# One work list for a skewed Fourier convolution: groups overlapped sequence by sequence

## The chip, the cores and the metric

The kernel runs on one core of one Trainium2 chip. The core has a matrix engine (PE, with PEld for its weight loads), a vector engine (DVE), a scalar engine (ACT), a general engine (POOL) and a queue engine (SP); DMA queues are issued from SP, POOL and ACT. The metric is the device time of one execution in microseconds (us). Before the change it is 2036.44 us, the median of three runs (2035.06 to 2037.47).

## The reference, cut to what matters

The work is a long causal convolution over 5696 positions for 8 sequences and 128 channels, followed by a token-mixing block. Its second part takes the first part's output as x.

```python
def _attn_ref(x, h):                       # x (8, 5696, 128), h (5696, 128)
    B, S, D = x.shape
    L = 2 * S
    Xf = np.fft.rfft(x, n=L, axis=1)
    Hf = np.fft.rfft(h, n=L, axis=0)
    return np.fft.irfft(Xf * Hf[None], n=L, axis=1)[:, :S, :]

def _moe_ref(x, w_theta, w_tok_r, w_tok_i, w_ch):
    theta = x @ w_theta
    zr, zi = x * np.cos(theta), x * np.sin(theta)
    y = np.einsum('ts,bsd->btd', w_tok_r, zr) + np.einsum('ts,bsd->btd', w_tok_i, zi)
    u = x + y
    return u + np.maximum(u @ w_ch, 0.0)
```

## The kernel before, in words

The convolution is computed as matrix products with tables of sines and cosines, in float16. The 8 sequences and 128 channels are cut into eight groups (`groups`): two sequences times 64 channels each, first the four pairs of sequences for the lower channels (dh = 0), then for the upper (dh = 1). A group goes through four stages, each a list of steps. A step fills one PSUM tile `ps` (two banks; there are four such tiles, so all eight banks) and copies it out.

- Stage A (`stage_a`, line 239): 16 steps of 4 matmuls of 180 columns, table `f1_t` times the loaded `x16`. Each result is copied to the tile `a` by ACT (line 258) or, for steps named in `on_dve`, by DVE (line 256).
- Stage B (`stage_b`, line 392): 12 steps (11 of 8 frequencies, one of 2). `f2` (line 261) makes the spectrum of both sequences e in one `ps`; ACT copies it to a tile `xs` (line 399; two buffers); DVE multiplies it with the real and the imaginary part of the filter's spectrum, held in `hs` tiles, into `u_t` and `v_t` (line 401). So `u_t` holds both sequences' products with one part of the filter, `v_t` with the other. In the last step `f2` issues twelve further matmuls (`WARM`, line 275) whose results nobody reads.
- Stage C (`stage_c`, line 411): 16 steps of 8 pairs of matmuls, table `r_u` with `u_t` and `r_v` with `v_t`; steps 0 to 7 belong to the first sequence of the pair, 8 to 15 to the second. The result is multiplied by a table of signs and halves, `sgn`, on its way to the tile `g`: on DVE in one instruction (line 429), or on ACT in two (lines 426 and 427).
- Stage D (`stage_d`, line 432): 7 steps (six of 10 positions, one of 4), table `e_t` times `g`, copied by ACT to `yt` (line 447). The last step stores `yt` to `yt_hbm` through SP (line 453).

There is one buffer each of `a`, `g`, `yt` and `x16`, and one pair `u_t`, `v_t`. The loop over groups (line 755) weaves stage C of group g with stage A of group g+1, and then stage B of group g+1 with stage D of group g (`woven` sorts the steps of several lists by a position in each). Stage C of g+1 can begin only when stage B of g+1 has written all of `u_t` and `v_t`, and stage B only when stage C of g has read all of them. When A has taken its last input, POOL loads the next group's `x16` (16 DMAs, line 138). In group 3's stage B, SP refills each `hs` tile with the upper channels' spectrum from `hf_hbm` (lines 405 to 408).

The order of the instructions on an engine is set in one of two ways. Inside `tc.manual_schedule` (here `in_order`) DVE and ACT take their instructions as the program writes them. Outside it, and always for PE, a planner orders them from its own costs and readiness. `in_order` ends after stage C of group 0 (line 770).

Group 7 has no following group. Its stages C and D are woven with the first steps of the phases (`phase_step`, line 715), which turn `yt_hbm` into the sines and cosines of the second part. They use small tables `ones`, `pm` and `w_neg`, made in `open_phases` (line 640) while group 6 is worked on, and `ya0`, loaded by POOL from `yt_hbm` (line 653). After the spectrum of group 7, the ring for the token-mixing weights takes the place of the table `w_t2` (`open_ring`, line 609). From about 400 us the mixing products (line 1262 above all) fill the rest of the time.

Of the kernel before, what the change touches and what calls it, by code (L numbers as in the profile page):

```python
# [23 lines left out]
def kernel(  # L24
# [42 lines left out]
    w_ch_sb = const_pool.tile([P, P], BF16)  # L67

# [9 lines left out]
    NF = 2 * S  # L78
    N2 = 64
    N1 = NF // N2  # L80
    NB = S // N2
    K1 = N1 // 2 + 1
    KH = K1 // 2
    CK = 8
    HD = D // 2
    EN = N2 // 2 + 1
    WARM = 12
    XP = HD + 4
    assert N1 * N2 == NF and NB * N2 == S and NB % 2 == 1 and K1 <= P
# [4 lines left out]
    UVW = 2 * HD * K1  # L94
# [9 lines left out]
    conv, setup, xa, xin, pha = (ExitStack() for _ in range(5))  # L104
# [10 lines left out]
    fs = pool("fft_s", 2, conv, side="right")  # L115
    fy = pool("fft_y", 1, conv, side="right")
    s1 = pool("set_1", 1, setup, side="right")

    u_t = fc.tile([P, UVW + P], F16)
    v_t = fc.tile([P, UVW + P], F16)  # L120
    uv = [t[:, :UVW].rearrange("p (e d k) -> p e d k", e=2, k=K1) for t in (u_t, v_t)]
    h16 = s1.tile([P, 2, N2, HD], F16)
    for p0, p1 in ((0, 80), (80, NB)):
        nc.gpsimd.dma_start(u_t[p0:p1, :N2 * D],
                            bass.AP(tensor=h.tensor, offset=h.offset + p0 * N2 * D,
                                    ap=[[N2 * D, p1 - p0], [1, N2 * D]]))
# [25 lines left out]
    nc.vector.memset(lane[0:64, 2:3], 0.0)  # L152
    nc.vector.memset(lane[64:P, 2:3], float(KH))

# [64 lines left out]
    nc.vector.tensor_scalar(lane[:, 3:4], lane[:, 0:1], 1.0 / NF, None, op0=mult)  # L219
# [6 lines left out]
    nc.vector.tensor_scalar(f_t, f_k, lane[:NB, 1:2], 1.0 / N1, op0=mult, op1=mult)  # L226
# [15 lines left out]
    def stage_a(lhs, on_dve=()):  # L242
# [3 lines left out]
        def chunk(q):  # L246
# [8 lines left out]
            if q // 4 in on_dve:  # L255
                nc.vector.tensor_copy(a_out, a_in)
            else:
                nc.scalar.activation(a_out, a_in, AF.Copy)
        return [lambda q=q: chunk(q) for q in range(0, HD, 4)], st

    def f2(a_st, c, warm=True):
# [11 lines left out]
        if c == NCK - 1 and warm:  # L273
            for n in range(WARM):
                nc.tensor.matmul(ps[:, n % 2, ck * HD:ck * HD + 384], w_t2[:, 2, :P],
                                 w_t2[:, 0:2, :].rearrange("p k n -> p (k n)"), start=True, stop=True)
# [14 lines left out]
    for d0 in range(0, HD, 32):  # L291
        nc.vector.tensor_copy(h16[:NB, :, :, d0:d0 + 32],
                              u_t[:NB, :N2 * D].rearrange("p (n h d) -> p h n d", h=2, d=HD)[:, :, :, d0:d0 + 32])
    steps, a_h = stage_a(lambda q: h16[:NB].rearrange("p h n d -> p (h n) d")[:, :, q], (4, 6, 8, 10, 12, 14))
    w_rest(1)
    for f in steps:
        f()
    w_rest(2)

    nc.gpsimd.memset(u_t[:, UVW:], 0.0)  # L300
    nc.gpsimd.memset(v_t[:, UVW:], 0.0)
# [22 lines left out]
    def h_chunk(c):  # L324
        c0, ck = CHK[c]
        ps = f2(a_h, c, False)
        nc.scalar.activation(h_part(c)[:, 0], ps[:, 0], AF.Copy, scale=16.0 / NF)
        nc.vector.tensor_scalar(h_later[:, HD * c0:HD * (c0 + ck)].rearrange("p (d k) -> p d k", k=ck),
                                ps[:, 1], 16.0 / NF, None, op0=mult)
# [13 lines left out]
    sgn = fc.tile([P, N2], F32)  # L343

    def r_table(n_, r_):
# [10 lines left out]
        nc.scalar.activation(r_[:, :N2 + EN], k[:, :N2 + EN], AF.Copy, scale=0.125)  # L356
        nc.scalar.activation(r_[:, N2 + EN:], k[:, N2 + EN:], AF.Copy, scale=-0.125)
# [7 lines left out]
    def e_pair(n, cn):  # L365
        at = e_more if n % 4 == 3 else e_all[:, 2 * (n % 4) * ES * NB:]
        return [at[:K1, q * ES * NB:][:, :cn * NB] for q in range(2)]

    def e_index(n, n0, cn):
        t, k = e_pair(n, cn)  # L370
        index(k, [[1, cn], [N2, NB]], n0)
        nc.gpsimd.tensor_scalar(t, k, lane[:K1, 1:2], 1.0 / NF, op0=mult, op1=mult)
        up(t, k, nc.gpsimd)

    def e_table(n, n0, cn):
# [4 lines left out]
        sine(e_t[:K1, n0:n0 + cn, 1, :], t3, -1)  # L380
        cosine(e_t[:K1, n0:n0 + cn, 0, :], k3)

    def s_table():
        half, end = lane[:, 5:6], lane[:, 6:7]
        nc.vector.tensor_scalar(half, lane[:, 1:2], 0.0, -0.5, op0=ALU.is_equal, op1=mult)
        nc.vector.tensor_scalar(end, lane[:, 1:2], float(K1 - 1), -0.5, op0=ALU.is_equal, op1=mult)
# [938 lines left out]
```

## Time and profile before

| | us |
|---|---|
| median of three runs | 2036.44 |
| the profiled execution | 2035.64 |
| its span | 2033.9 |
| PE busy | 1936.4 |
| DVE busy | 1573.3 |
| POOL busy | 964.0 |
| ACT busy | 655.1 |
| first stage A matmul of group 2 | at 108.34 |
| first matmul of the phases | at 334.98 |

The profile holds one execution. A busy PE is a modelled figure, because matmuls are pipelined, so the distance from one start to the next says more than a sum of durations. A group of instructions is written as line, engine, operation, output tile, input tile, shape and count; behind the bar stand the total busy time, the mean duration in nanoseconds, and the idle time of the engine just before them with what ended it. On one engine the next instruction often starts a little before the one before it ends, so the pitch is shorter than the duration.

### The profile page before, as it was taken

To read this page: it belongs to the slowest core of one execution; us is meant where nothing else is said; L and a number is where in the kernel's file an instruction comes from. 1 tells how busy PE (TensorE), PEld (TensorE's weight loads), DVE (VectorE), ACT (ScalarE), POOL (GpSimd) and SP (SyncE) were. 2 spreads that over 40 slices of the span, in tenths; PEclk is the share of its full clock that TensorE was granted. 3 is DMA by queue.
4 is the path that set the end of the run, shared out by engine and by line. 5 is a ranking of instruction groups with operands and counts; after the bars stand their busy time and mean duration, and the time that the engine had idled before them with its cause. 6 is when DMAs were issued, how large, how long until landed. Compare 5 with 4: busy or idle time off the path is not lost.

```text
span 2033.9 us, 41286 instructions
## 1 busy us (share of the span) xinstructions
PE 1936.4 (95%) x15664; PEld 1073.2 (53%) x15841; DVE 1573.3 (77%) x2890; ACT 655.1 (32%) x1004; POOL 964.0 (47%) x1721
## 2 busy tenths in 40 slices
PE   6799999788999999999999999999999999999998
PEld 5688888654444444444444444444444444444444
DVE  8777778786788888888877669768677786777767
ACT  6788888851232323333210000011111111111111
POOL 8523322363364545455565554553545445354450
PEclk9799999998999999999999999999999999999999
DMA  9978975997898998989999899887878878788793
GB/s 115 64 84 124 89 87 165 266 272 139 163 174 177 174 178 154 180 170 181 171 168 164 121 241 243 131 149 129 152 135 146 149 129 144 137 146 147 133 157 85
DMA packets 487752, 312.05 MB, mean 153 GB/s; under 512 B 182887, under 2 KB 448615, under 8 KB 486567
## 3 DMA queue, kind: packets, MB, share of 16 engines
q0 software_dynamic: 321600, 155.29, 60.8%
q1 hardware_dynamic: 158784, 140.34, 24.0%
q10 hardware_dynamic: 7168, 13.76, 1.9%
q8 instruction: 124, 2.03, 0.4%
q14 instruction: 76, 0.62, 0.1%
HBM read 354.37 MB, written 90.29 MB: 219 GB/s over the span
## 4 chain that ended last, share of the span: by engine, by line
PE 66%; DMA 3%; DVE 3%; issue 1%; POOL 0%; ACT 0%; DVEq 0%; ACTq 0%
PE m L1262 62%; DMA b<-z_hbm 2%; DVE c L1269 1%; PE v L942 1%; PE utp L935 1%; PE m L1266 1%; PE m L1150 1%; DVE wt L855 1%; PE theta_ps L515 0%; PE tpz L883 0%; DMA yT<-yt_hbm 0%; PE m L1183 0%; POOL ring L631 0%; DMA ring<-in_moe_w_tok_r_dram 0%; DMA ring<-in_moe_w_tok_i_dram 0%
## 5 line engine op out<-in xcount | busy, mean ns | idle before, releaser
L631 POOL DMA_DIRECT2D ring<-in_moe_w_tok_i_dram x720 | 390.2, 552 | 652.8 <-DVE wt L855 554.0
L855 DVE STREAM_TRANSPOSE wt<-ring 128x384 f32<-128x384 f32 (+2 forms) x720 | 358.9, 523 | 115.1 <-PE m L1262 63.7
L631 POOL DMA_DIRECT2D ring<-in_moe_w_tok_r_dram x720 | 388.5, 553 | 124.8 <-DVE wt L855 79.5
L1262 PE MATMUL m<-b,wt 128*128 128x512 bf16 x1605 | 384.8, 379 | 4.1 <-DVE wt L855 2.1
L1262 PEld LDWEIGHTS <-wt 128*128 128x128 bf16 x1804 | 176.0, 98 | 216.4 <-DVE wt L855 5.1
L1269 DVE TENSOR_TENSOR c<-c,m 128x512 f32<-128x512 f32 x412 | 265.3, 669 | 0.4 <-PE m L1262 0.4
L937 ACT ACTIVATE ring<-utp 128x512 bf16<-128x512 bf16 x85 | 50.8, 597 | 575.8 <-PE utp L935 575.8
L138 POOL DMA_DIRECT2D x<-in_x_dram x128 | 99.6, 807 | 140.4 <-PE ps L251 132.8
L421 PE MATMUL ps<-r_u,u_t 128*128 128x128 f16 x1024 | 124.6, 220 | 6.9 <-DVE u_t L401 3.5
L1183 PE MATMUL m<-b,wt 128*128 128x512 bf16 x471 | 113.1, 387 | 12.0 <-DMA b<-zr_hbm 8.1
L422 PE MATMUL ps<-r_v,v_t 128*128 128x128 f16 x1024 | 123.6, 220 | 0.3
L932 ACT ACTIVATE ub<-c 128x512 bf16<-128x512 f32 x88 | 55.1, 628 | 185.8 <-DMA ring<-in_moe_w_tok_i_dram 103.8
L422 PEld LDWEIGHTS <-v_t 128*128 128x128 f16 x1024 | 100.6, 98 | 5.6 <-issue 4.2
L421 PEld LDWEIGHTS <-u_t 128*128 128x128 f16 x1024 | 100.6, 98 | 4.7 <-DVE u_t L401 4.7
L399 ACT ACTIVATE xs<-ps 128x1024 f16<-128x1024 f32 x96 | 91.5, 982 | 8.8 <-PE ps L269 2.6
L1183 PEld LDWEIGHTS <-wt 128*128 128x128 bf16 x528 | 51.5, 99 | 71.0 <-issue 17.1
L401 DVE TENSOR_TENSOR u_t<-xs,hs 128x1024 f16<-128x1024 f16 x96 | 64.2, 669 | 31.7 <-ACT xs L399 29.3
L885 ACT ACTIVATE ring<-tpz 128x512 bf16<-128x512 bf16 (+1 forms) x46 | 27.5, 597 | 148.8 <-PE tpz L883 123.7
L517 ACT ACTIVATE red<-theta_ps,magic 128x512 f32<-128x512 f32 (+1 forms) x46 | 31.6, 687 | 127.1 <-PE theta_ps L515 99.4
L269 PEld LDWEIGHTS <-w_t 64*128 64x128 f16 x3240 | 60.4, 102 | 22.0 <-issue 15.8
L401 DVE TENSOR_TENSOR v_t<-xs,hs 128x1024 f16<-128x1024 f16 x96 | 63.7, 664 | 0.0
L944 DVE SCALAR_TENSOR_TENSOR c<-v,c 128x512 f32<-128x512 f32 x88 | 59.9, 682 | 2.9 <-PE v L942 2.6
(2932 smaller groups left out, 3773.3 us busy)
## 6 DMA issues: line engine op xcount, KB each, us to landing
ring<-in_moe_w_tok_r_dram POOLq DMA_DIRECT2D x352, 96.0 KB, 4.6
ring<-in_moe_w_tok_i_dram POOLq DMA_DIRECT2D x352, 96.0 KB, 4.9
ring<-in_moe_w_tok_r_dram POOLq DMA_DIRECT2D x352, 80.0 KB, 4.4
ring<-in_moe_w_tok_i_dram POOLq DMA_DIRECT2D x352, 80.0 KB, 3.8
cp_hbm<-c SPq DMA_DIRECT2D x88, 256.0 KB, 2.3
c<-cp_hbm SPq DMA_DIRECT2D x88, 256.0 KB, 4.5
out_dram<-c SPq DMA_DIRECT2D x88, 256.0 KB, 4.2
yy<-y_hbm SPq DMA_DIRECT2D x84, 128.0 KB, 2.5
```

The costliest lines, as they stand in the source:

```text
L138: nc.gpsimd.dma_start(x16[p0:p1, e, n0:n0 + 16, :HD], bass.AP(tensor=src.tensor, offset=src.offset + (p0 * N2 + n0) * D + dh * HD, ap=[[N2 ...
L269: nc.tensor.matmul(ps[:, e, j * HD:(j + 1) * HD], w_t2[rows, slot(e, c0 + j), N2 * (1 - ri):N2 * (3 - ri)], a_st["a"][rows, ri * K1 + c0 + ...
L399: nc.scalar.activation(xs[:, :, :, :ck], ps, AF.Copy)
L401: nc.vector.tensor_tensor(uv[r][:, :, :, c0:c0 + ck], xs[:, :, :, :ck], hv[:, r:r + 1].to_broadcast([P, 2, HD, ck]), op=mult)
L421: nc.tensor.matmul(o, u_t[:, at:at + P], r_u, start=True, stop=False)
L422: nc.tensor.matmul(o, v_t[:, at:at + P], r_v, start=False, stop=True)
L631: nc.gpsimd.dma_start(wb[32 * i:32 * i + 32, :ng, :nj * 64], bass.AP(tensor=a.tensor, offset=a.offset + row0 * S + p * H + i * QR + j0 * 6 ...
L855: nc.vector.transpose(wt.rearrange("p j t r -> p (j t r)").bitcast(F32).rearrange("p (j g t) -> p g j t", j=TJ, g=4)[:, :ng, :nj], wb[:, : ...
L944: nc.vector.scalar_tensor_tensor(c[:m], v[:m], 0.0, c[:m], op0=ALU.max, op1=ALU.add)
L1183: nc.tensor.matmul(ms[n // 2 * 2 + h], a[n][:, j, :, r], bts_of[p][jj][n % 2 * 2 + h][:, r, :], start=(n % 2 == 0 and jj == 0 and r == 0), ...
L1262: nc.tensor.matmul(ms[q], a[q][:, j, :, r], bts[jj][q][:, r, :], start=(jj == 0 and r == 0), stop=(jj == NJ - 1 and r == 1 and q not in left))
L1269: nc.vector.tensor_tensor(c, z, ms[q], op=op)
```

## The change

The transform is taken at frequencies shifted by a quarter of a bin (`QUARTER`), over 5696 instead of 11392 points. The tables `w_t2`, `f1_t`, `e_t` and `r_u`, `r_v` are computed for these frequencies; the number and shape of matmuls in stages A to D stay as they were, except that C and D use 89 partitions of `g` instead of 90. The first and last frequency need no halving and the signs move into the tables, so `sgn` and its six instructions go, and stage C's results are copied plainly, by ACT or DVE in one instruction.

The product tiles are now one per sequence: `uv_t[0]` and `uv_t[1]`, each with both parts of the filter. A spectrum step and its products become separate pieces: `spectrum(c)` makes `xs` (three buffers instead of two), `products(c, e)` writes sequence e's products, with `xs` repeated over the two parts of the filter where before the filter was repeated over the two sequences. The instruction's element count is the same. The twelve extra matmuls of `f2` go.

For groups 0 to 6 the order is written out as a string, `PLAN`, of which each letter is one piece: a, c, d are steps of stages A (of group g+1), C and D (of group g) copied out by ACT, and A, C, D the same copied by DVE; f is a spectrum of group g+1, p its products for the first sequence, q for the second, and r the last three products of the second sequence, carried over from the list before. In group 0, C and A stay woven as before and the list is taken for the remaining letters. ACT and DVE keep the program's order until the last group begins. After the last A step the next x is loaded.

In the last group the three late products come first, then phases and stage C as before. The tables `ones` and `w_neg` move into the ring's small area, and `open_phases` is called after the list of group 6, when the ring is open. `ya0` is loaded without its last 128 columns, which SP loads to a place of their own.

```diff
+    QUARTER = 0.25
-    WARM = 12
-    fs = pool("fft_s", 2, conv, side="right")
+    fs = pool("fft_s", 3, conv, side="right")
-    u_t = fc.tile([P, UVW + P], F16)
-    v_t = fc.tile([P, UVW + P], F16)
+    uv_t = [fc.tile([P, 2, UVP], F16, name=f"uv{e}") for e in range(2)]
...
-        if c == NCK - 1 and warm:
-            for n in range(WARM):
-                nc.tensor.matmul(ps[:, n % 2, ck * HD:ck * HD + 384], w_t2[:, 2, :P], ...
-    def stage_b(a_st, warm, refill):
+    def stage_b(a_st, refill):
+        xs_of, made = {}, [0] * NCK
+        def spectrum(c):
+            ps = f2(a_st, c)
+            xs = xs_of[c] = fs.tile([P, 2, HD, CK], F16, tag="xs", name="xs")
+            nc.scalar.activation(xs[:, :, :, :CHK[c][1]], ps, AF.Copy)
+        def products(c, e):
             c0, ck = CHK[c]
-            for r in range(2):
-                nc.vector.tensor_tensor(
-                    uv[r][:, :, :, c0:c0 + ck], xs[:, :, :, :ck],
-                    hv[:, r:r + 1].to_broadcast([P, 2, HD, ck]), op=mult)
-            if refill:
+            nc.vector.tensor_tensor(
+                uv[e][:, :, :, c0:c0 + ck],
+                xs_of[c][:, e:e + 1, :, :ck].to_broadcast([P, 2, HD, ck]), h_part(c), op=mult)
+            made[c] += 1
+            if refill and made[c] == 2:
...
-                nc.tensor.matmul(o, u_t[:, at:at + P], r_u, start=True, stop=False)
-                nc.tensor.matmul(o, v_t[:, at:at + P], r_v, start=False, stop=True)
+                e, d = divmod(8 * n + i, HD)
+                for r, r_ in enumerate((r_u, r_v)):
+                    nc.tensor.matmul(o, uv_t[e][:, r, d * K1:d * K1 + P], r_, start=(r == 0), stop=(r == 1))
-            if q % 16 == 0 and (last or q >= 64):
-                nc.scalar.mul(g_out[:, :, :EN], g_in[:, :, :EN], sgn[:K1, 0:1])
-                nc.scalar.mul(g_out[:, :, EN:], g_in[:, :, EN:], sgn[:K1, EN:EN + 1])
-            else:
-                nc.vector.tensor_tensor(g_out, g_in, sg, op=mult)
+            if on_dve:
+                nc.vector.tensor_copy(g_out, g_in)
+            else:
+                nc.scalar.activation(g_out, g_in, AF.Copy)
...
+    PLAN = "aaaAcrAaCaccrArcAacAacAacAcaAcCfCfcpfpCpccqqqfffqpqdfppqffdqpdqpDffpdqfpdpDp"
+    LATE = PLAN.count("r")
+    def ready_for_phases():
+        xin.close()
+        sides["phases"] = {}
+        load_ya0()
+    def run_plan(plan, g, a_chunk, c_chunk, d_chunk, spectrum, products, late_products):
+        at = {"a": 0, "c": 0, "d": 0, "f": 0, "p": 0, "q": 0, "r": NCK - LATE}
+        for x in plan:
+            k = x.lower()
+            n, at[k] = at[k], at[k] + 1
+            if k == "f":
+                spectrum(n)
+            elif k in "pq":
+                products(n, "pq".index(k))
+            elif k == "r":
+                late_products(n, 1)
+            else:
+                {"a": a_chunk, "c": c_chunk, "d": d_chunk}[k](n, x.isupper())
+            if k == "a" and at[k] == NA:
+                if g + 2 < len(groups):
+                    load_x(g + 2)
+                else:
+                    ready_for_phases()
...
+        if g + 1 == len(groups):
+            in_order.close()
             late_order.enter_context(tc.manual_schedule(engines={mybir.EngineType.Pool}))
+            for c in range(NCK - LATE, NCK):
+                late_products(c, 1)
             for _ in range(3):
                 steps0.pop(0)()
...
+        if g == 0:
+            woven((steps_of(c_chunk, NC, [n for n in range(NC) if n % 2 or n < 8]), 0.06, 1.0),
+                  (steps_of(a_chunk, NA, (5, 11)) + [lambda: load_x(2)], 0.0, 0.55), (e_left, 0.0, 0.9))
             first.close()
+            plan = [x for x in PLAN if x in "fpqdD"]
+        run_plan(plan, g, a_chunk, c_chunk, d_chunk, spectrum, products, late_products)
+        late_products = products
         if g + 2 == len(groups):
             load_ya1()
             open_ring()
+            open_phases()
+            load_ya0_end()
```

## The prediction

> **What bounds the kernel now.** I read the page's shares and its forty slices first, then the tensor-engine timeline of the convolution to find its rhythm, then busy time by stretch, then the costliest groups with their shapes kept apart, and last the timelines of ACT and PE inside one stretch. From the page, the busy line and the slices (51 us each):
>
> ```profile
> PE 1936.4 (95%) x15664; PEld 1073.2 (53%) x15841; DVE 1573.3 (77%) x2890; ACT 655.1 (32%) x1004; POOL 964.0 (47%) x1721
> ...
> PE   6799999788999999999999999999999999999998
> ...
> DVE  8777778786788888888877669768677786777767
> ACT  6788888851232323333210000011111111111111
> ...
> PEclk9799999998999999999999999999999999999999
> ```
>
> PE is busy nearly everywhere, but ACT is full only in the first eight slices, some 400 us. That is the Fourier convolution, and the diff touches little outside it. The first matmuls of stage A (line 251) of groups 2 to 7 start at 108.34, 145.42, 185.37, 223.40, 260.22 and 297.43 us; the first transpose of the phases comes at 334.98. Between them lie six like periods: inverse C of group g woven with A of g+1, then spectrum B of g+1 woven with inverse D of g. Busy time in these stretches:
>
> ```profile
> core 0: us, PE busy (x) PEld busy (x) DVE busy (x) ACT busy (x) POOL busy (x), PEclk, DMA share, GB/s
> 108.34:145.42 37.08, 34.49 (x826) 32.04 (x822) 29.05 (x36) 32.34 (x43) 12.00 (x16) 1.00 0.83 82
> 145.42:185.37 39.95, 35.62 (x825) 33.24 (x822) 30.29 (x38) 32.95 (x45) 12.03 (x16) 0.96 0.95 120
> 185.37:223.40 38.03, 35.41 (x824) 33.19 (x822) 28.39 (x36) 32.55 (x44) 12.02 (x16) 0.96 0.98 111
> 223.40:260.22 36.82, 34.12 (x825) 31.86 (x822) 28.77 (x36) 32.36 (x43) 12.03 (x16) 1.00 0.83 83
> 260.22:297.43 37.21, 34.45 (x825) 32.02 (x822) 29.11 (x36) 32.45 (x44) 12.04 (x16) 1.00 0.82 82
> 297.43:334.98 37.55, 34.50 (x824) 32.10 (x822) 29.28 (x39) 32.59 (x44) 3.63 (x5) 1.00 0.41 122
> ```
>
> The columns are length, PE, PEld, DVE, ACT and POOL busy (count), granted clock, DMA. The mean is 226.64 / 6 = 37.77 us. No engine fills a period: ACT 32.5 and DVE 29.2 of 37.8, and PE's 34.8 holds modelled overlaps. The loss is in the hand-over between two halves with different limits. The evictions, same stretch, by form:
>
> ```profile
> L399 ACT ACTIVATE xs<-ps 128x1024 f16<-128x1024 f32 x67 | 67.3, 1035 | 2.7 <-PE ps L269 1.0 <-ACT g__2352 L427 0.3 <-ACT g__3336 L427 0.3
> ...
> L401 DVE TENSOR_TENSOR u_t<-xs,hs 128x1024 f16<-128x1024 f16 x67 | 46.3, 691 | 20.3 <-ACT xs L399 18.4
> ...
> L429 DVE TENSOR_TENSOR g__7308<-ps,sgn 90x1024 f16<-90x1024 f32 x12 | 14.6, 1221 | 5.1 <-PE ps L422 5.1
> ...
> L258 ACT ACTIVATE a__6305<-ps 128x720 f16<-128x720 f32 x16 | 11.6, 771 | 2.0 <-PE ps L251 1.5
> ...
> L426 ACT ACTIVATE g__7308<-ps,sgn 90x528 f16<-90x528 f32 x4 | 2.8, 697 | 1.7 <-PE ps L422 1.6
> ```
>
> The reader is to see the wait behind each bar: products (line 401) wait for ACT's xs, C's evictions (line 429) for PE. So B/D is bound by ACT and C/A by PE. Pitches are from the timelines, ACT's for instance:
>
> ```profile
> 330.57 0.93 ACT L447 ACTIVATE yt<-ps 128x890 bf16<-128x890 f32 x1
> 331.38 1.95 ACT L399 ACTIVATE xs<-ps 128x1024 f16<-128x1024 f32 x2
> 333.19 0.95 ACT L447 ACTIVATE yt<-ps 128x890 bf16<-128x890 f32 x1
> ```
>
> A yt copy starts 0.81 after the one before it began to hold ACT; two xs copies take 1.81, so 0.91 each. Likewise, per piece: PE takes 0.32 for an A step (70.80 to 71.12), 0.89 for a C step, 0.52 for a spectrum step (64 matmuls in 1.04), 0.95 for a D step (169.50 to 170.45); ACT 0.72 for A; DVE 0.895 for A, 1.22 for C, 0.605 for a product.
>
> **Before, in halves.** C/A on PE: 16 x 0.32 + 16 x 0.89 = 19.4. B/D on ACT: 11 x 0.91 + 0.36 + 6 x 0.81 + 0.36 = 15.6. Sum 35.0; the four periods at full clock average 37.17, so hand-overs cost 2.1.
>
> **The work list, one period.** ACT gets 8 a, 12 c, 12 f and 5 d: 5.8 + 10.9 + 10.4 + 4.1 = 31.1. DVE gets 8 A, 4 C, 24 products (two short, 0.34) and 2 D (scaled by elements from the 720-element cast: 1.08 and 0.50): 7.2 + 4.9 + 14.0 + 1.6 = 27.6. PE: 19.4 + 5.9 + 6.1 = 31.4, without the twelve warming matmuls of line 275 (1.96). The chain that sets the period: the second products (q) overwrite what C steps 8 to 15 read, and only three xs tiles exist, so f3 waits for q0 and q0 for the last C. Behind f3 on ACT stand f4, f5 and d0, behind q0 on DVE q1 to q3 and p3; PE waits for both through the ps tiles. Up to the last C, PE issues 16 A, 16 C and three f, 20.9, its first steps lying beside the previous period's end; with the four ps tiles walked through by these pitches that C ends at 20.7 after ACT's first copy. Then ACT still has one C, nine f and five d: 0.9 + 8 x 0.91 + 0.36 + 4.05 = 12.6. With one handover of 0.15: 33.5. DVE's 12.2 behind the same C (9 p, 9 q, two D) fits beside it. To this come waits: none gives 33.5, all of before's 2.1 gives 35.6; I take the middle, 34.5, since A now begins under D's end but the order of ACT and DVE is fixed. Six periods: 6 x (37.77 - 34.5) = **-19.6** (bounds -25.6 and -13.0).
>
> Two prices inside are not shown. C on ACT as one copy of 1024 elements: the xs copy of the same size takes 0.91, the two halves of lines 426 and 427 take 1.14 together; the first is nearest (one instruction, same count). The other end adds 12 x 0.23 = 2.8 to ACT's sum, 33.9, of which some 0.2 to 2.8 lands. A product whose xs, not hs, is repeated: 0.605 as now, or 1.22 as the rows of 1024 elements with float32; I take the first, because types, counts and the inner run of eight stay.
>
> **Other parts.** *Sign.* Six small DVE instructions (lines 385 to 390) took 48.10 to 48.97; DVE waited 1.81 for xs soon after, so nothing lands. Two new ones on lane cost about 0.15 each at the start. Together 0 (-0.9 to +0.3). *Group 0's C/A:* ACT runs without a gap from 83.7 to 92 us; four pairs become single copies, 4 x 0.23: **-1.0** (-1.0 to 0). *Spectrum of group 1, which has no C beside it:* ACT worked from 91.9 to A at 108.34; now two copies go to DVE (-1.2), but three spectra come before any q and ACT waits 1.3 for q0, and the warming goes: **-0.5** (-1.5 to +1.5). *Group 7:* ACT is almost gapless from 345 to 380 and loses 8 x 0.23 = 1.8; in front DVE gains three late products, 1.55, and the memset of ones, 0.17, beside which POOL's w_neg (0.54) now follows the last spectrum instead of standing free at 311. The first transposes need neither. **-1.0** (-1.8 to +2.3). *DMA queues.* On SP, three refills of three DMAs each move to the next list's start, behind the yt stores, which before were queued behind refills until 195.0; the next reader is 20 us off and they land in 3.4. yt is written again some 22 us after its store, landing 6.7. The last 128 columns of ya go to SP: 128 KB, nearest row 8.1 to land, read last of 22 tiles. On POOL the ya load is shorter and comes after the same A. What comes closest to showing is x: 16 issues on POOL begin when A ends, take 12.0 (once 14.4) and land 4.7 to 6.9 later. With A ending at 12.9 that is 12.9 + 0.3 + 12.0 + 6.9 = 32.1, still under 34.5; before it had 6 us of slack. It is the next floor.
>
> **Sum.** -19.6 - 1.0 - 0.5 - 1.0 = -22.1. The profiled execution took 2035.64 (span 2033.9 and 1.7 around it), 0.8 under the median 2036.44. 2035.64 - 22.1 = 2013.5, or on the median's footing **2014.3**.
>
> **The clock, weighed.** With warming gone I looked at PE just before the slow stretch of the second period:
>
> ```profile
> 173.75 1.10 PE L269 MATMUL ps<-a__3317,w_t 64*128 64x64 f16 x63 [1.11 <-issue]
> 174.79 0.99 PE L444 MATMUL ps<-e_t,g__3336 90*128 90x89 f16 x20
> ...
> 178.58 0.46 PE L444 MATMUL ps<-e_t,g__3336 90*128 90x89 f16 x7 [1.59 <-issue]
> ...
> 180.38 1.68 PE L444 MATMUL ps<-e_t,g__3336 90*128 90x89 f16 x20
> ```
>
> Twenty D matmuls took 1.68 instead of 0.99, after gaps of 1.11 and 1.59. The two periods with granted clock 0.96 average 38.99 against 37.17: a dip costs 1.8. In my walk no PE gap exceeds 0.6, so I charge nothing; if gaps of 1.1 return in each period, 6 x 1.8 = 10.9. [...]
>
> **Rivals.** *Dip in each period:* for it the gaps above, against it the denser list; 2014.3 + 10.9 = 2025. *x late:* with 14.4 of issue and 9.0 to land (the longest), the next A could start only at 12.9 + 0.3 + 14.4 + 9.0 = 36.6; five periods load x, 5 x 2.1 = 10.5, 2025. Against: five of six loads took 12. *The fixed order stalls (slower):* ACT and DVE now take their work strictly as written in every period, with four ps and three xs tiles. Where ACT's next copy is not ready, it holds all behind it. Place: ACT's 37 copies a period; price: 0.30, the gap that each C eviction on DVE shows today ("5.1 <-PE" over ten). 33.5 + 37 x 0.30 = 44.6, +60: 2075. It decides from 0.13 a copy, where the period is 38.2. For it: in the first spectrum, ordered that way already, DVE waits 1.81 twice for xs. Against: ACT's A copies run six and nine in a row without a wait, and the running sums of PE and ACT along the list stay within 1.5 up to c15. *Products at 1.22 (slower):* DVE 27.6 + 14.8 = 42.4 a period, 2014 + 47 = 2061; nothing in the rows speaks for it but the new operand. *The gain is made in the periods and lost in the phases and mixing, which are planned anew:* DMA shares are near 1.0 from 334 to 430; no change, 2036.
>
> **Chances.** Forecast 0.58 (own range 2006 to 2024), dip 0.10, x late 0.10, no change 0.05, fixed order 0.13, products 0.04. Faster by over 0.2% (4.1 us, about what this measurement can tell): 0.58 + 0.10 + 0.10 = 0.78; same 0.05; slower 0.17. The lower end takes all waits at none (33.5) and the gains' far bounds: 2036.4 - 25.6 - 4.3 = 2006. The upper end reaches past the two partial gains toward no change, 2034; outside lie 0.17 above and some 0.03 below.
>
> **What would show it.** Right: first A to first A at 33.5 to 35.6; ACT over 0.9 of it; C copies near 1.03 long on ACT; products still near 0.69 long; granted clock 1.00. Wrong: A waiting for an x DMA, products over 0.8, many short ACT waits on PE, or PE waits over 1 us before spectra. The prediction falls if ACT and DVE are found waiting in turn for each other at every step, or if the time saved by 335 us is gone again at 430.

## The result, and the profile after

The changed kernel takes **2022.09 us** (median of six executions, 2018.64 to 2024.96), the kernel before 2036.43 beside it (six, 2034.26 to 2037.47). The ratio is 0.993, with a 95% interval of 0.9918 to 0.9943: faster by 14.3 us, where the forecast had 22.1. The executions of the changed kernel lie further apart than those of before, and the profiled one, 2024.96 (span 2023.2), is the slowest of its six; against before's 2035.64 its traces have only 10.7 us to share out.

The busy line and the slices of the page of after, which answer to those of before:

```profile
PE 1929.2 (95%) x15581; PEld 1073.0 (53%) x15757; DVE 1565.0 (77%) x2900; ACT 646.2 (32%) x954; POOL 963.8 (48%) x1721
...
PE   5799998889999999999999999999999999999998
...
DVE  8877778776788888888877668777677776877767
ACT  6788998742232323232300000011111111111111
...
PEclk9789999899999999999999999999999999999999
```

PE has lost 7 us of busy time, DVE 8 and ACT 9. In the lines shown no digit differs by more than one; the granted clock is now at 8 in the third and in the eighth slice, where before had 9, and at 9 in the tenth, where before had 8. The stretches between the first matmuls of stage A (line 255) of groups 2 to 7 and the first transpose of the phases, by window, with the last part of group 1's spectrum in front (columns: length, PE, PEld, DVE, ACT, POOL busy with counts, granted clock, DMA share, GB/s):

```profile
89.80:108.39 18.59, 16.24 (x424) 15.01 (x418) 13.54 (x21) 14.34 (x18) 3.25 (x5) 0.68 0.62 41
108.39:144.36 35.97, 34.49 (x811) 33.23 (x810) 27.68 (x38) 31.44 (x37) 11.95 (x16) 0.93 0.85 84
144.36:180.46 36.10, 33.75 (x810) 32.35 (x809) 27.89 (x39) 31.86 (x38) 11.94 (x16) 0.95 1.01 121
180.46:217.86 37.40, 33.61 (x809) 32.06 (x808) 27.87 (x38) 32.26 (x39) 11.96 (x16) 0.95 0.98 124
217.86:251.69 33.83, 32.35 (x812) 30.89 (x810) 27.62 (x38) 31.58 (x38) 11.98 (x16) 1.00 0.90 90
251.69:285.35 33.66, 32.30 (x813) 30.95 (x810) 27.67 (x38) 31.32 (x37) 12.01 (x16) 1.00 0.91 90
285.35:320.75 35.40, 33.44 (x809) 32.05 (x808) 27.68 (x38) 31.87 (x38) 4.07 (x5) 0.95 0.42 122
```

The first row is not a period. The six periods are 35.97, 36.10, 37.40, 33.83, 33.66 and 35.40: sum 212.36 where before had 226.64, mean 35.39. The two at clock 1.00 last 33.7 and the other four, at 0.93 to 0.95, 36.2. DVE does 27.7 and ACT 31.3 to 32.3 a period, so in the short periods ACT is busy 0.93 of the time.

The costliest evictions of the same stretch, by form:

```profile
L398 DVE TENSOR_TENSOR uv<-xs,hs 128x1024 f16<-128x1024 f16 x133 | 84.1, 684 | 3.0 <-ACT xs L394 1.8 <-PE ps L419 0.2
L394 ACT ACTIVATE xs<-ps 128x1024 f16<-128x1024 f32 x67 | 65.5, 1030 | 9.7 <-PE ps L278 6.5 <-ACT g__4297 L425 0.5 <-ACT g__2334 L425 0.5
...
L449 ACT ACTIVATE yt<-ps 128x890 bf16<-128x890 f32 x31 | 28.4, 935 | 3.8 <-PE ps L443 3.8
...
L425 ACT ACTIVATE g__7210<-ps 89x1024 f16<-89x1024 f32 x12 | 12.1, 1022 | 1.1 <-PE ps L419 1.0
...
L260 DVE CAST a__7185<-ps 128x720 f16<-128x720 f32 x8 | 7.3, 907 | 3.8 <-PE ps L255 3.8
```

The waits behind the bars have moved. Products (line 398, both tiles in one row now) waited 18.4 us for ACT's xs in the first tile's row alone and now wait 1.8; copies of C on ACT are single ones of 1.02, products are still 0.68. ACT's spectrum copies now wait for PE, 6.5. What PE itself waits for in the six periods, from the table of waits, is nearly all one thing:

```profile
PE ps L278 <- issue: 5.8, 7, 1.5
PE ps L443 <- issue: 5.1, 3, 2.0
PE ps L255 <- ACT yt L449: 0.9, 3, 0.3
PE ps L278 <- ACT xs L394: 0.5, 2, 0.3
```

"Issue" means that no semaphore, tile or transfer in the profile held PE. One such place in the third period, PE's timeline (start, length, operation, count, and in brackets the idle time before and its releaser):

```profile
204.20 0.68 PE L443 MATMUL ps<-e_t,g__4297 89*128 89x89 f16 x12
206.86 0.50 PE L443 MATMUL ps<-e_t,g__4297 89*128 89x89 f16 x8 [1.98 <-issue]
207.29 1.57 PE L278 MATMUL ps<-a__4272,w_t 64*128 64x64 f16 x96
208.80 1.19 PE L443 MATMUL ps<-e_t,g__4297 89*128 89x89 f16 x24
211.41 2.10 PE L443 MATMUL ps<-e_t,g__4297 89*128 89x89 f16 x36 [1.43 <-issue]
```

From one stop to the next PE passes 8 + 96 + 24 = 128 matmuls, each with its weight load: 256 instructions. The other pairs give the same: 62 + 60 + 6 between 171.09 and 177.01, 18 + 60 + 50 between 244.46 and 249.01, 60 + 60 + 8 between 277.66 and 281.94. Before has them too, 63 + 20 + 32 + 13 between 173.75 and 178.58. The view of the DMA queues names a transfer of that rhythm, in the first five periods (packets, MB, share):

```profile
q8 instruction: 31, 0.51, 1.1%
```

In these 177 us PE has 4055 matmul and 4047 weight-load records, 8102 / 256 = 31.6 blocks, and the instruction queue 31 packets of 0.51 / 31 MB = 16.5 KB: about one packet for every 256 instructions of PE. Where spectra and D steps mix, two such restarts lie 4.3 to 5.9 us apart; C steps (16 matmuls in 0.89) use up a block in 8 x 0.89 = 7.1 us, and no stop of after lies among them. My reading, an inference that no view shows directly, is that PE arrives at the end of a block before the next one has landed; the runs below test it.

The traces also hold the time of every packet. Around the first stop of the timeline above, from 203.5 to 206.8, POOL's queue, which carries x, and the instruction queue show (packets, MB, share):

```profile
q0 software_dynamic: 2819, 0.32, 161.1%
q8 instruction: 1, 0.02, 2.3%
```

The one instruction packet began at 204.13 and took 1.21 (2.3% of 16 engines' 3.3 us), and PE went on 1.5 after its end. In all twelve kernels of this document there are 113 stops with the releaser issue between 60 and 332 us, and every one ends 1.2 to 1.8 us after the end of an instruction packet. How soon the next packet begins after such a restart depends on x: in the 50 cases in which no packet of POOL's queue began in between, it took 1.04 to 1.87 (43 times under 1.25); in the 20 cases in which it took longer, 1.9 to 4.8, between 1055 and 3976 packets of that queue had begun first. (In before, from 211.88 on, 1577 of them began in between and it still took 1.68, as little as without.)

The rest of the time, by landmarks, after less before: up to the start of group 2's A +0.05; six periods -14.28; from the phases' first transpose to the first mixing product 56.6 before and 59.2 after, +2.6; from there to the end +0.9. Together -10.7, of which only the periods are a gain.

### The profile page after: what moved, and what is told of

It is laid out like the page before. It is cut to its first block, busy times and chain, and to the rows that moved or that the text cites. A ratio compares the mean times of both kernels' runs of the same rounds, so it can differ in the third digit from the quotient of the medians.

```text
span 2023.2 us, 41078 instructions
## 1 busy us (share of the span) xinstructions
PE 1929.2 (95%) x15581; PEld 1073.0 (53%) x15757; DVE 1565.0 (77%) x2900; ACT 646.2 (32%) x954; POOL 963.8 (48%) x1721
## 4 chain that ended last, share of the span: by engine, by line
PE 64%; DVE 4%; DMA 2%; issue 2%; POOL 1%; ACT 0%; DVEq 0%; SPq 0%; POOLq 0%
PE m L1305 59%; DVE c L1312 2%; PE v L985 1%; PE utp L978 1%; POOL ring L640 1%; PE m L1309 1%; DVE wt L898 1%; PE m L1193 1%; DMA b<-z_hbm 1%; DMA ring<-in_moe_w_tok_r_dram 0%; PE theta_ps L524 0%; PE tpz L926 0%; DMA yT<-yt_hbm 0%; DMA c<-cp_hbm 0%; DMA cp_hbm<-c 0%
## 5 line engine op out<-in xcount | busy, mean ns | idle before, releaser
L419 PE MATMUL ps<-r_u,uv 128*128 128x128 f16 x1024 | 126.8, 221 | 4.1 <-DVE g__1336 L423 1.2
L419 PE MATMUL ps<-r_v,uv 128*128 128x128 f16 x1024 | 126.3, 221 | 0.0
L398 DVE TENSOR_TENSOR uv<-xs,hs 128x1024 f16<-128x1024 f16 (+1 forms) x192 | 116.7, 661 | 10.4 <-ACT xs L394 9.3
L419 PEld LDWEIGHTS <-uv 128*128 128x128 f16 x2048 | 121.3, 99 | 6.0 <-issue 3.9
L526 ACT ACTIVATE red<-theta_ps,magic 128x512 f32<-128x512 f32 (+1 forms) x46 | 31.6, 687 | 129.4 <-PE theta_ps L524 98.2
L255 PE MATMUL ps<-f_t,x 89*128 89x180 f16 x512 | 56.0, 251 | 7.7 <-DMA x<-in_x_dram 4.8
L831 DVE TENSOR_TENSOR b<-b 128x1024 bf16<-128x1024 bf16 x100 | 61.3, 679 | 0.0
```

Source lines behind the costliest of these rows:

```text
L398: nc.vector.tensor_tensor(uv[e][:, :, :, c0:c0 + ck], xs_of[c][:, e:e + 1, :, :ck].to_broadcast([P, 2, HD, ck]), h_part(c), op=mult)
L419: nc.tensor.matmul(o, uv_t[e][:, r, d * K1:d * K1 + P], r_, start=(r == 0), stop=(r == 1))
L831: return [lambda f=f, x=x: f(*x) for f, x in ((nc.vector.tensor_sub, (bt[M3], b12, b22)), (nc.vector.tensor_sub, (bt[M4], b21, b11)), (nc. ...
```

## The experiments

All ratios are to the kernel before, run on the same chip. Times of the kernel before in the three groups of runs: 2037.68, 2036.94 and 2036.64. "Stops" are PE's idle times before which no releaser but issue stands, summed over the convolution: 11.5 us before, 12.2 after.

**The constant of the phases made earlier (e1).** At 323 us in after, PE's first product of the phases needs ones, which DVE writes behind the last products of the list (seven in one row, and a short one), and ACT waits for what follows:

```profile
320.85 0.93 ACT L449 ACTIVATE yt<-ps 128x890 bf16<-128x890 f32 x1
324.96 0.60 ACT L546 ACTIVATE ph<-ps 128x512 f32<-128x512 f32 x1 [3.18 <-DVE ring L744]
```

```profile
318.32 4.08 DVE L398 TENSOR_TENSOR uv<-xs,hs 128x1024 f16<-128x1024 f16 x7
...
323.10 0.17 DVE L652 MEMSET ring<- 128x128 bf16 x1
...
324.50 0.43 DVE L744 COPY ring<-ps 128x512 bf16<-128x512 bf16 x1 [1.22 <-PE ps L541]
```

(ACT first, DVE below it; the last line of each is what comes out late.) The edit moves the opening of the ring and of the phases up to the last spectrum in group 6's list:

```
-            open_ring()
-            open_phases()
             load_ya0_end()
...
                 spectrum(n)
+                if g + 2 == len(groups) and n == NCK - 1:
+                    open_ring()
+                    open_phases()
```

> The changed kernel, with the memsets of ones and pm and w_neg placed right after the last spectrum of group 6's list instead of after its last product. Theory (the table of ones stands on DVE behind the last products, and the first phases wait for it: ACT idle 3.18 us before its first phases copy, against 1.53 before the change): the gap shrinks by 1.5 to 2 us and the time falls by as much, to about 2020.3. Rival (the first phases wait for something else, such as the late products that DVE takes there): no change, 2022.

Measured: 2024.89 (seven executions, 2019.67 to 2034.96), ratio 0.9945 (0.9925 to 0.9965). The wait itself shrank, from 3.18 to 1.88:

```profile
323.09 0.94 ACT L449 ACTIVATE yt<-ps 128x890 bf16<-128x890 f32 x1
325.90 0.60 ACT L546 ACTIVATE ph<-ps 128x512 f32<-128x512 f32 x1 [1.88 <-DVE ring L744]
```

But the phases up to the first mixing product took 63.1 us, not 59.2. From the phases' first transpose to the end it is 1702.8, against 1702.4 in after, so the 1.3 taken from the wait did not reach the end in this execution; the rest of its time is in the six periods, 215.8 against 212.4. The median can't tell a gain of 1.3, since its interval is 4 us either way. The wait is real, and nothing shows that the end hangs on it.

**The list without its skew (e2).** Same tiles, same split between ACT and DVE, but the order of before: A with C, then spectra, products and D.

```
-    PLAN = "aaaAcrAaCaccrArcAacAcAacAcaAcCfCfcpfpCpccqqqfffqpqdfppqffdqpdqpDffpdqfpdpDp"
+    PLAN = "aaaAcAaCaccAcAacAcAacAcaAcCCcCccffpqfpqdfpqfpqdfpqdfpqfpqDfpqfpqdfpqdfpqpqD"
```

> The changed kernel with the list rearranged only: all A and C of a period first, then spectrum, both products and D in turn, no late products; same tables, product tiles, copies and fixed order. Theory (the skew makes the gain, by letting ACT's and DVE's evictions of the next spectrum begin before the last inverse): at full clock C/A is 19.4 on PE, then products and two D copies on DVE 15.6, with hand-overs of 2.1 about 37.1 a period against 33.7, six periods: +20, 2042. Rival (the plain copies, the even split of evictions and the missing signs make the gain, not the order): within 4 us of the changed kernel, 2022.

Measured: 2036.06, ratio 0.9994 (0.9981 to 1.0008). Without the skew nothing is left of the gain. Its periods sum to 229.01. The one at clock 1.00, from 218.65 to 254.82, lasts 36.17 where after's last 33.7: 2.5 a period, or 15 of the 16.7 that the six take more; the rest may come from its more stops (15.1 us in all). ACT's waits for C come back, in the table of waits of this kernel (the C copies of one group a line) 26.0 us over six groups, where after has 7.4:

```profile
ACT g__7213 L425 <- PE ps L419: 5.7, 6, 2.4
ACT g__6245 L425 <- PE ps L419: 4.7, 5, 2.0
ACT g__2337 L425 <- PE ps L419: 4.3, 5, 1.6
ACT g__4309 L425 <- PE ps L419: 4.1, 5, 1.6
ACT g__5277 L425 <- PE ps L419: 3.9, 6, 1.6
ACT g__3305 L425 <- PE ps L419: 3.3, 6, 1.6
```

**The planner in place of the written order (e3).** The order of DVE and ACT is released when the periods begin.

```
+            in_order.close()
             first.close()
```

> The changed kernel, but ACT and DVE keep the program's order only up to group 0's inverse, as before the change; from there the planner orders them, given the same list as its priorities. Theory (the written order is worth something only together with the skew; the planner knows ready times by its own costs): some of the gain is lost, period 34.5 to 36, +5 to +13: 2027 to 2035. Rival (a fixed order costs waits that a planner avoids): faster than 2022 by 2 to 6.

Measured: 2021.46, ratio 0.9924 (0.9907 to 0.9941). The intervals of this and of the change overlap almost wholly: given the list as the order of emission, holding two engines to it neither gains nor costs that can be seen, so both the loss and the gain that were weighed failed to come.

**The warming matmuls put back (e4).** Behind the last spectrum step of groups 1 to 7:

```
+        if c == NCK - 1 and warm:
+            for n in range(12):
+                nc.tensor.matmul(ps[:, n % 2, ck * HD:ck * HD + 384], w_t2[:, 2, :P],
+                                 w_t2[:, 0:2, :].rearrange("p k n -> p (k n)"), start=True, stop=True)
...
```

> The changed kernel with the twelve warming matmuls put back behind the last spectrum step of each group from 1 on; nothing else. Theory (the lower granted clock in four of the six periods follows gaps in the middle of PE's steps, where PE waits for nothing that the profile shows; the warming comes after them): no better, 2022 to 2027, since 1.96 of PE time comes back where D's last two steps and the next A wait. Rival (the clock falls because the warming is gone): periods return to 33.7 each, 6 to 10 less, 2012 to 2016.

Measured: 2029.02, ratio 0.9964 (0.995 to 0.9979). Windows of its first four periods:

```profile
107.75:144.82 37.07, 35.41 (x824) 33.33 (x822) 27.76 (x38) 31.80 (x38) 11.99 (x16) 0.95 0.83 82
144.82:181.36 36.54, 34.03 (x825) 31.93 (x823) 27.67 (x38) 31.84 (x38) 11.99 (x16) 1.00 1.00 124
181.36:217.51 36.15, 34.20 (x824) 32.00 (x822) 27.67 (x38) 31.96 (x38) 11.99 (x16) 1.00 0.99 124
217.51:253.70 36.19, 34.03 (x824) 31.94 (x822) 27.92 (x38) 31.94 (x38) 11.99 (x16) 1.00 0.85 84
```

The clock is 1.00 in four of six periods, two more than in after, but these now last 35.2 to 36.5, on the mean 36.0, where an undisturbed one lasts 33.7: with the twelve matmuls, of 1.96 us, a period is 2.3 longer. The stops stay, 10.9 us in all. The time is 2 us over the expected range. Taking the warming out was right: a period with it costs about as much as a dip.

**No x loads for groups 3 to 7 (e5).** These groups compute on group 2's data; five of the eight loads are left out.

```
+        if g >= 3:
+            x16s[g] = x16s[2]
+            return
```

> The changed kernel without the loads of x for groups 3 to 7, which work on group 2's x instead: this part of the input is left out, and with it 5 of the 8 loads. What it tells: PE stops one to three times a period in the middle of a step, always 128 matmul pairs (256 instructions) apart, and waits for nothing that the profile shows (0.4 to 2.0 us each, 12 us in the convolution). Theory A (its instructions come late, and they are late because their transfer shares the DMA engines with the small packets of x): with x gone the stops of groups 2 to 6 fall under 0.5 us each, clock 1.00 in all periods, periods 33.5 to 33.8, so 6 to 9 less: about 2014. Theory B (they are late because the spectrum and D steps use up 256 instructions faster than the next come, whatever the traffic): stops of 0.5 to 2 us stay, clock dips stay, time within 3 us of 2022.

Measured: **2012.28** (2010.06 to 2013.86), ratio 0.9876 (0.9863 to 0.9888). Its six windows:

```profile
107.03:140.74 33.71, 32.63 (x809) 31.24 (x808) 27.72 (x40) 31.46 (x39) 0.00 (x0) 1.00 0.20 46
140.74:174.46 33.72, 32.63 (x809) 31.19 (x808) 27.59 (x39) 31.48 (x39) 0.00 (x0) 1.00 0.33 81
174.46:208.16 33.70, 32.54 (x809) 31.16 (x808) 27.58 (x39) 31.46 (x38) 0.00 (x0) 1.00 0.39 100
208.16:241.86 33.70, 32.66 (x809) 31.23 (x808) 27.59 (x39) 31.46 (x38) 0.00 (x0) 1.00 0.20 47
241.86:275.56 33.70, 32.59 (x809) 31.22 (x808) 27.59 (x39) 31.46 (x38) 0.00 (x0) 1.00 0.20 46
275.56:309.91 34.35, 32.16 (x808) 30.77 (x808) 27.56 (x38) 31.68 (x38) 4.05 (x5) 1.00 0.42 126
```

Five periods fall to 33.7 and the sixth, which has no x load in after either, to 34.35, all at clock 1.00, and PE's waits for issue in the six fall from 10.9 to 2.6:

```profile
PE ps L281 <- issue: 2.0, 3, 1.3
...
PE ps L446 <- issue: 0.6, 1, 0.6
```

That next to nothing of it is a wait for x data is shown by after itself, whose two undisturbed periods last 33.83 and 33.66 with the loads in place. So transfers that PE doesn't wait for cost it some 10 us, by way of its instruction stops and the lower clock behind them.

**Half of D's matmuls (e6).** One of the two matmuls of each D output is left out, and with it half of each sum.

```
-                for ri in range(2):
+                for ri in range(1):
...
-                    nc.tensor.matmul(o, g_[:N1, ri * N2 + n, :], e_, start=(ri == 0), stop=(ri == 1))
+                    nc.tensor.matmul(o, g_[:N1, ri * N2 + n, :], e_, start=True, stop=True)
```

> The changed kernel with one of the two matmuls of each pair in stage D left out, so that half of the inverse's sum is missing: 64 pairs of instructions and 3 us of PE less per period, all in the stretch where PE has time to spare; copies and products stay. Theory (that stretch is paced by ACT behind the last C, at full clock): a period with full clock stays at 33.5 to 33.8; the stops get rarer or shorter, with fewer instructions, and the dips with them, total 2013 to 2020. Rival (PE paces that stretch): periods fall by up to 3, 2004 or less.

Measured: 2022.23, ratio 0.9921 (0.9907 to 0.9935), as the change itself. Its best two periods are 33.70 and 33.71, as with all of D, so PE's work doesn't set the period. The expected 2013 to 2020 was missed: the stops are fewer, 8.4 us, but three are of 1.4 and more, the granted clock is 0.82 to 0.95 in all six periods, and the longest lasts 38.14.

**A fourth D copy on ACT (e7).**

```
-    PLAN = "aaaAcrAaCaccrArcAacAcAacAcaAcCfCfcpfpCpccqqqfffqpqdfppqffdqpdqpDffpdqfpdpDp"
+    PLAN = "aaaAcrAaCaccrArcAacAcAacAcaAcCfCfcpfpCpccqqqfffqpqdfppqffdqpdqpdffpdqfpdpDp"
```

> The changed kernel with the fourth D copy of each list moved from DVE to ACT. Theory (the chain is PE up to the last C, then ACT's copies, 12.6 us): ACT's part grows by 0.81, a period at full clock goes from 33.7 to 34.5, six periods and the first spectrum's list: +5, 2027. Rival (ACT has room behind the last C): no change, 2022.

Measured: 2026.24, ratio 0.9948 (0.9934 to 0.9961), 4 us more than the change, as expected. One copy of 0.81 more on ACT in each period is 6 x 0.81 = 4.9. Its two periods at clock 1.00 last 34.26 and 34.84. With e6, in which less work on PE left the shortest period as it was, this says that ACT sets an undisturbed period.

**Fill on PE in front of the fast steps (e8).** Three matmuls of 384 columns ahead of four D steps of each list, meant, by the reading above, to give the next block of instructions time to land.

```
+            fill = FILL if not then and n in (1, 2, 3, 4) else 0
...
+            for i in range(fill):
+                nc.tensor.matmul(ps[:, i % 2, :384], w_t2[:, 2, :P],
+                                 w_t2[:, 0:2, :].rearrange("p k n -> p (k n)"), start=True, stop=True)
```

> The changed kernel with three extra matmuls of 384 columns (0.16 us each) ahead of D's steps 1 to 4 in every list, written into the tile that D then overwrites: 1.9 us of PE more per period, where PE otherwise waits for a free tile. Theory (the clock falls when PE has been idle for a good part of some microseconds; PE's time is spare there): granted clock 1.00 in all or all but one of the periods, periods at 33.7 plus what the stops cost directly, 2015 to 2019. Rival (the fill lies on the path, as the warming did in the run before): 2024 to 2032.

Measured: 2028.3, ratio 0.9958 (0.9944 to 0.9971). Stops 7.9 us, and the clock 1.00 in five of six periods; but those five last 35.2 on the mean, 1.5 over the undisturbed 33.7. With the fill PE stops less and pays more for it than the stops cost, as the rival said.

**A first, so that x is loaded earlier (e9).** All of A ahead of most of C, the rest of the list as it was.

```
-    PLAN = "aaaAcrAaCaccrArcAacAcAacAcaAcCfCfcpfpCpccqqqfffqpqdfppqffdqpdqpDffpdqfpdpDp"
+    PLAN = "aaAaArAacAraAaAcraAacAcCcCccccfCfcpfpCpccqqqfffqpqdfppqffdqpdqpDffpdqfpdpDp"
```

> The first part of the list is reordered only: the sixteen A steps and the three late products are taken as early as the two evicting engines allow (two on ACT for one or two on DVE), three C steps among them, the other eight C steps behind. By the pitches the last A ends some 8.5 us into the period instead of 12.9, so the 16 issues of the x load run from 8.5 to 20.5 and land by 26, where they ran from 12.9 and landed by 30. The fast part of the period (spectra and D) begins at 17. Theory (x packets on the shared DMA engines delay the fetch of PE's instructions): the overlap shrinks from about 13 us to 9, so about a third of the 10 us that leaving the loads out gained comes back: 2022 - 3.5 = 2018 to 2020, stops of PE 8 to 10 us in all instead of 12.4. Rival (the order of the front part is what sets the period: with A in front DVE carries 9.0 us of A and late products before C, and PE waits for ps tiles): each period 0.5 to 1.5 us longer, 2025 to 2031, stops as before.

Measured: 2022.82, ratio 0.9932 (0.9918 to 0.9945): nothing gained and nothing lost, but both halves of it are in the windows (the second to the fourth period):

```profile
141.40:176.21 34.81, 33.16 (x809) 31.43 (x808) 27.12 (x39) 31.47 (x39) 12.01 (x16) 1.00 1.00 118
176.21:216.50 40.29, 34.94 (x809) 32.94 (x809) 27.18 (x39) 31.84 (x39) 12.01 (x16) 0.96 0.98 122
216.50:251.57 35.07, 32.83 (x809) 31.13 (x808) 27.04 (x38) 31.59 (x38) 12.03 (x16) 1.00 0.87 87
```

The x load now begins 10 us into the period where it began at 14. Five of six periods have clock 1.00, and the stops sum to 6.9 us, close to half. And each of the five lasts 34.81 to 35.07, since ACT waits for C (0.77 twice in a period) once it has no A copies left to put between them: 1.2 x 6 = 7. The sixth, 40.29, holds stops of 1.54 and 2.52. The time is in neither range, and each of the two was half right: with the load earlier the stops are fewer, and the order in front does cost, by about the same amount.

**x in large runs (e10).** The same 16 issues and nearly the same bytes, but each partition's run of 1024 numbers is read and written as one of 1088. The tile is filled with other numbers than it should hold.

```
+                    if g >= 3:
+                        nc.gpsimd.dma_start(
+                            x16[p0:p1, e].rearrange("p n d -> p (n d)")[:, n0 * XP:(n0 + 16) * XP],
+                            bass.AP(tensor=src.tensor, offset=src.offset + (p0 * N2 + n0) * D + dh * HD,
+                                    ap=[[N2 * D, p1 - p0], [1, 16 * XP]]))
+                        continue
```

> The x loads of groups 3 to 7 keep their 16 issues, their place and about their bytes (1088 numbers for 1024 in each partition's run), but each run is contiguous in DRAM and in the tile, where it was 16 rows of 64 numbers: a sixteenth or less of the packets. The tile is filled with other numbers than the kernel needs, so the output of these groups is left wrong. Theory (many small packets are what PE's instruction fetch queues behind): near the time with the loads left out, 2012 to 2015, clock 1.00, periods 33.7 to 34.5. Rival (any x transfer of these bytes, or the issuing itself, does it): 2020 to 2024, stops of 12 us in all as before.

Measured: 2017.37 (2015.81 to 2019.95), ratio 0.9905 (0.9891 to 0.9918), midway between the change and e5. POOL's queue in the first five periods, of after and of this kernel:

```profile
q0 software_dynamic: 62720, 7.31, 67.3%
```

```profile
q0 software_dynamic: 5120, 7.75, 28.7%
```

A twelfth of the packets and 0.42 of their time; POOL's issuing fell too, from 12.0 to 8.3 us a period. Stops still sum to 11.0 us in the profiled execution (2019.95, the slowest of the four), and two of its periods have clock 0.91. The time lies between the theory's 2012 to 2015 and the rival's 2020 to 2024, so neither holds alone: less work for the DMA engines (or on POOL, which this run doesn't part from it) helps, but nearly the same bytes in large runs still disturb.

## Why the prediction was right, and where its size was off

*The direction and its cause* were right: the hand-over between two halves with different limits was what the change took away (e2: without the skew 2036.06).

*The period.* The walk of the list gave 33.5 without waits. The undisturbed periods of after, e5 and e6 are 33.7, within 0.2. "I take the middle, 34.5" added 1.0 for waits between ACT and DVE in the written order; these are 0.2. The mean came to 35.39, so the term of the sum, -19.6, measured **-14.28**, inside its bounds of -25.6 and -13.0. That it stayed inside is luck: the upper bound allowed for hand-overs between engines, and what filled it was stops of PE and the lower clock. Likewise the measured 2022.09 lies inside the stated range but nearer to 2025, the price of the dips, than to 2014.3. With the x loads out the same term is 202.88 - 226.64 = -23.8. (DVE's "12.2 behind the same C" adds up to 11.9 from its own prices, 16 x 0.605 + 2 x 0.34 + 1.08 + 0.50; nothing hangs on it.)

*The step that failed* is in "The clock, weighed": "In my walk no PE gap exceeds 0.6, so I charge nothing". The walk knows only work and semaphores, and the gaps of 1.11 and 1.59 that I showed in before were not gaps in the work. Both said "<-issue"; counting the matmuls between them (63 + 20 + 32 + 13 = 128) would have shown a rhythm of the instructions and not of the order, a reason to expect that they stay. They stayed: 9.7 us in the stretch of before, 10.9 in after. The price per dip, 1.8, was low: the four dipped periods of after average 36.2 against 33.75, 2.5 each. "Dip in each period", priced at 10.9 and given a chance of 0.10, came in four of six periods and made 4 x 2.5 = 10 of the difference to 33.7.

How long a stop stands before a dip can be counted. By the stops after 100 us that begin at full clock, of before, after and all experiments but e6, the granted clock over the next 6 us was below 0.8 in 19 of the 32 cases where PE had stopped for 1.40 us or longer, and in none of the 61 where it had stopped for less. (In e6, where PE has less work around its stops, it was so in all three cases of 1.40 or longer, and behind one stop of 0.85.) The longest of the 32 is 2.83, and 1.40 was enough. It is no limit for the whole convolution: before 100 us, in the same kernels, the clock was 0.63 to 0.70 behind five of eight stops shorter than 1.40, these five of 0.47 to 1.35.

*Prices.* C on ACT as one copy: 1.02 long, as taken. Products with the other operand repeated: 0.68, as taken, and the rival at 1.22 fell. ACT 31.1 a period: 31.3 to 31.6 undisturbed. DVE 27.6: 27.7. *The warming* is worth 1.5 to 2.8 a period (e4), around the 1.96 that was counted.

*x late* was not seen in the periods: after's A starts are 33.7 apart with the loads in place, and the floor was put at 32.1. It was the same load that cost the time, in another way (2012.28 without five of the eight in e5). The prediction looked at when x lands and not at whom its packets pass.

*DMA queues* were hidden, as said: refills land in 3.3 to 3.6 us, yt's stores in 6.6, and among PE's waits in the six periods there is no transfer.

*The fixed order stalls* fell: e3 without it is 2021.46, ACT's waits are short, and DVE's too. Its price of 0.30 for each of ACT's 37 copies would have been 11.1 a period; ACT is idle for 2.3 in an undisturbed one.

*Group 0's C/A and group 1's spectrum*, -1.5 together: +0.05. A of group 1 began 0.7 later (a wait of 4.83 for its x where before had 2.3), and a stop of 1.35 that ended at 94.61 was followed by a granted clock of 0.56 up to 114.00, into the first period. In e2 and e3 the clock was 1.00 there, and group 2's A began at 102.58 and 103.59: here too the dip is larger than the terms of the sum.

*Group 7 and the phases*, -1.0 (-1.8 to +2.3): +2.6. "The first transposes need neither" ones nor w_neg was true of the transposes, but the first product with them (line 535) follows at once, and ACT behind it waits 3.18 where it waited 1.53. That is 1.65 of it, and in e1's execution taking 1.3 of this wait away didn't bring the end forward. In e2, e3, e5 and e7 to e10, which change nothing in it, this stretch took 57.5 to 61.9 us, never before's 56.6, and from the first transpose to the end they took 1699.7 to 1702.3 where before took 1698.9; so some of the rest is scatter and some is the change's, and which part of it stays open.

*What is shown and what is argued.* That the x loads cost the time is shown by e5, and that making them lighter gives half of it back by e10. That the stops come every 256 PE instructions is shown by the counts, and that each ends 1.2 to 1.8 us after an instruction packet by the packets' times. That x's packets delay the next instruction packet rests on e5 and on the 20 late ones, all of which had over a thousand of them in between, where none was as late without. Open is why large runs of x, with far fewer packets, still leave stops, and what decides whether a stop of 1.40 or longer brings a dip. A load of x that is spread out more thinly was not tried.

## What to carry to other kernels

A walk through a list by pitches predicted the undisturbed period within 0.2 us; what it can't see are stops whose releaser is "issue". Where such stops stand in the trace of before, count the instructions between them: if the count is constant, as the 256 here, compare the stops' ends with the packets of the instruction queue; here a denser list of short matmuls kept them. Here many small packets cost time on an engine that never waited for them, so the place of a transfer beside PE's fastest stretch deserves a term in the sum, with the whole load left out as the bound (here 10 us).

## What the hardware showed that was not expected

- PE stops 256 instructions apart among spectra and D steps, with restarts 4.3 to 5.9 us apart in after: 0.4 to 2.0 us each, up to 2.8 in e3, one or two in a period, 10.9 us in six periods; 2.6 with the x loads left out. Each of 113 such stops ended 1.2 to 1.8 us after a packet of the instruction queue (16.5 KB). Behind a restart the next packet began 1.0 us later at the soonest, and up to 4.8 us later with x packets in front.
- The granted clock fell below 0.8 behind 19 of 32 single stops of 1.40 to 2.83 us and behind none of 61 shorter ones (after 100 us and from full clock, e6 apart); before 100 us it did so behind five of eight stops shorter than 1.40. A period with stops of 1.54 and 2.52 took 40.29 in e9, 5.4 more than its neighbours: the two stops are 4.1 of it.
- Nearly the same bytes (7.75 for 7.31 MB) by the same number of issues, in a twelfth of the packets, took 0.42 of the DMA engines' time (28.7% against 67.3%), and the kernel's time fell by half of what leaving them out gave.
